# Cosformer attention and a low-rank mixer on one core: batch 1's loads without a gate, fewer zero matmuls at the start, one normalisation moved

## The chip, the cores and the metric

The kernel runs on one core of a Trainium2 chip. The metric is the device time of one execution in microseconds, as the median of several runs. The kernel before took 336.32 us as the median of 5 runs, which lay between 334.65 and 339.53 us.

## The reference

Two layers follow each other, for 8 batches of 576 positions. The first is a linear attention with 8 heads of 64 features, the second a token mixer of rank 32 with a channel network of 2048 hidden units.

```python
theta = np.pi / 2.0 * pos / S                       # S = 576
phi(x) = concat([relu(x) * cos(theta), relu(x) * sin(theta)])      # 64 -> 128 features
kv  = einsum('bhsf,bhsd->bhfd', phi(k), v);  z = sum(phi(k), axis=2)
x   = einsum('bhsf,bhfd->bhsd', phi(q), kv) / (einsum('bhsf,bhf->bhs', phi(q), z) + 1e-06)
u   = x + transpose(transpose(x) @ U @ V)           # mixes the 576 positions, rank 32
out = u + relu(u @ w_ch1) @ w_ch2                   # 512 -> 2048 -> 512
```

All inputs and the output are float32. The kernel computes in bfloat16 and accumulates in float32.

## The kernel before, in words

**Tiling.** A batch's 576 positions are four chunks of 128 (c = 0 to 3) and a tail of 64 (c = 4). The order ORD takes the tail first. Two consecutive batches form a pair, and their tails share one tile. The time goes to the channel network: `g1_main` is its first product (four matmuls of 512 columns for each of 16 blocks j of 128 hidden units), `g2_part` its second. For every batch but the first two, the attention is spread over slots between these products, by a plan written out as slot numbers.

**The order is written by hand.** Each engine works through its instructions in the order in which the program issues them, so a late operand holds all that is queued behind it on that engine. The loads of q, k and v are issued on the queue of SyncE (SP), one after the other. The weights w_ch1 (`w1_load`, four parts of 512 hidden units) and w_ch2 are loaded through the queue of GpSimd (POOL), which converts them to bfloat16 on the way.

**Batch 0** has nothing to hide behind. The stages are: zero matmuls on TensorE while the loads run (`keep_warm`, L669); `q_prep`, the scaled relu of q on VectorE (DVE) and ScalarE (ACT); five units of eight transposes each (`qtr_unit`, L673), each followed by one zero matmul and a copy out of PSUM; `k_prep`; thirteen zero matmuls (L677); then the chain. `chain_head` casts v, forms kv for heads 0 to 3, their denominators and reciprocals (`den_unit`, whose result is called rec), and normalises the five chunks for these heads (`xh_unit`: four small matmuls, then a multiplication on DVE). `chain_mid` does the same for heads 4 to 7, and puts between the second and the third of its five normalisations the opening of two products for the mixer (`uTd_open`, L646), the first half of the product with U (`A_unit`, L648) and its follow-up with V (`uTd_mm`, L650). `chain_end` does the second half of the product with U, which needs all five normalised chunks of heads 4 to 7.

**Batch 1** runs beside the sixteen blocks `g1_main(0, j)` of batch 0: after block j = 0 to 4 comes a `q_prep`, after j = 2 to 6 a `qtr_unit`, after j = 6 and 7 the `k_prep`, and after j = 7 the chain, in which `fill1` places the blocks j = 8 to 12.

**Gates.** Three small operations hold loads back. On POOL a copy of one element of k (L679 for batch 0, L715 for batch 1) stands ahead of the weight loads, so that these start only when k has landed. On SP a tiny transfer of one element of rec stands ahead of batch 1's nine loads (L685), and one of batch 1's rec ahead of batch 2's (L642, for b = 1). SP cannot issue what is behind such a transfer until rec exists. The buffers of q and v are single, so their next load also waits for the last reader; those of k are double.

Of the kernel before, what the change touches and what calls it, by code (L numbers as in the profile page):

```python
# [17 lines left out]
def kernel(  # L18
# [11 lines left out]
    nc = tc.nc  # L30
# [18 lines left out]
    def tail(b):  # L49
        lo = TS * (b % 2)  # L50
        return slice(lo, lo + TS)
# [37 lines left out]
    def w1_load(n):  # L89
        cs = slice(n * 512, n * 512 + 512)  # L90
        nc.gpsimd.dma_start(
            out=w1_bf[:, :, cs], in_=moe_w_ch1.rearrange("(d p) n -> p d n", p=P)[:, :, cs]
        )
# [7 lines left out]
    def cast(eng, o, i):  # L101
# [6 lines left out]
    V_, A_, G_ = nc.vector, nc.scalar, nc.gpsimd  # L108
# [9 lines left out]
        out=iota[:, 0:4], pattern=[[1, 4]], base=0, channel_multiplier=4,  # L118
        allow_small_or_imprecise_dtypes=True,
    )  # L120
    for lo in (0, TS):
        nc.gpsimd.iota(
            out=iota[lo : lo + TS, 4:5], pattern=[[1, 1]], base=512, channel_multiplier=1,
# [11 lines left out]
        out=stU[:, 0:4, :], in_=moe_U[0:512, :].rearrange("(p c) r -> p c r", c=4)  # L135
# [33 lines left out]
    def keep_warm(n, tag, bufs):  # L169
        w_ps = ps.tile([P, 512], FP32, tag=tag, bufs=bufs, name="w_ps")  # L170
        for _ in range(n):
            nc.tensor.matmul(out=w_ps, lhsT=zero[:, 0:P], rhs=zero, start=True, stop=True)  # L172
# [4 lines left out]
    mark2 = const.tile([1, 1], FP32)  # L177
# [13 lines left out]
    def v_prep(b, h0=0, h1=H, cs=range(5), engs=None):  # L191
        vx = v_ext[b % 2]
        for n, c in enumerate(cs):
            eng = engs[n] if engs else G_
            if eng is None:
                continue
            if c < 4:
                cast(eng, vx[:, c, h0:h1, 0:D], vst[b][:, h0:h1, c, :])
            else:
                cast(eng, vx[tail(b), 4, h0:h1, 0:D], vt[b][tail(b), h0:h1, :])  # L200

    def v_block(b, h0, h1, c0, c1, eng):
        cast(
            eng,
            v_ext[b % 2][:, c0:c1, h0:h1, 0:D].rearrange("p c h d -> p h c d"),
            vst[b][:, h0:h1, c0:c1, :],
        )
# [29 lines left out]
    def kv_unit(b, hg, tag, bufs, eng=None):  # L237
        if b not in kv_sb:
            kv_sb[b] = pool.tile([P, H, E], BF16, tag="kv", bufs=2, name="kv")
        acc = ps.tile([P, 4, E], FP32, tag=tag, bufs=bufs, name="kv_ps")  # L240
        vx = v_ext[b % 2]
        for i in range(4):
            h = hg * 4 + i
            for c in range(5):
                nc.tensor.matmul(  # L245
                    out=acc[:, i, :],
                    lhsT=k_p[b][:, c, h, :] if c < 4 else k_tl[:, h, :],
                    rhs=vx[:, c, h, :],
                    start=(c == 0),
                    stop=(c == 4),  # L250
                )
        cast(eng or V_, kv_sb[b][:, hg * 4 : hg * 4 + 4, :], acc)
# [32 lines left out]
    def qT_of(b, c, h):  # L285
        return q_pT[b][:, c, h, :] if c < 4 else q_tlT[:, h, :]

    def x_alloc(b):
        if b not in x_bf:
            x_bf[b] = pool.tile([P, 4, DM], BF16, tag="x_bf", bufs=2, name="x_bf")  # L290

    def x_of(b, c, rows=slice(0, P)):
        return x_bf[b][:, c, :] if c < 4 else x_tl[rows, :]

    def recip(rec, den):
        nc.vector.tensor_scalar(out=rec, in0=den, scalar1=1e-6, scalar2=None, op0=ALU.add)  # L296
        nc.vector.reciprocal(out=rec, in_=rec)  # L297

    def den_unit(b, h0, h1, tag, bufs):
        n = h1 - h0  # L300
        d_ps = ps.tile([P, 5, n], FP32, tag=tag, bufs=bufs, name="d_ps")
        for c in range(5):
            for h in range(h0, h1):
                nc.tensor.matmul(
                    out=d_ps[:, c, h - h0 : h - h0 + 1],
                    lhsT=qT_of(b, c, h),
                    rhs=kv_sb[b][:, h, D:E],
                    start=True,
                    stop=True,
                )  # L310
        rec = pool.tile([P, 5, n], FP32, tag="rec5", bufs=2, name="rec5")
        recip(rec, d_ps)
        return rec

    def xh_unit(b, c, h0, h1, rec, tag, bufs):
        x_alloc(b)
        n = h1 - h0
        rows = slice(0, P) if c < 4 else tail(b)
        acc = ps.tile([P, n, D], FP32, tag=tag, bufs=bufs, name="xh_ps")
        for h in range(h0, h1):  # L320
            nc.tensor.matmul(
                out=acc[:, h - h0, :], lhsT=qT_of(b, c, h), rhs=kv_sb[b][:, h, 0:D],
                start=True, stop=True,
            )
        nc.vector.tensor_tensor(
            out=x_of(b, c, rows)[:, h0 * D : h1 * D].rearrange("p (i d) -> p i d", d=D),
            in0=acc[rows],
            in1=rec[rows, c, :].unsqueeze(2).to_broadcast([P if c < 4 else TS, n, D]),
            op=ALU.mult,
        )  # L330
# [28 lines left out]
    def A_unit(b, tag, bufs, eng=None, n0=0, n1=DM, a_ps=None):  # L359
        if b not in A_sb:  # L360
            A_sb[b] = pool.tile([P, DM], BF16, tag="A_sb", bufs=2, name="A_sb")
        if a_ps is None:
            a_ps = ps.tile([P, DM], FP32, tag=tag, bufs=bufs, name="a_ps")
        for c in range(5):
            nc.tensor.matmul(  # L365
                out=a_ps[:, n0:n1],
                lhsT=U_of(b, c),
                rhs=x_of(b, c)[:, n0:n1],
                start=(c == 0),
                stop=(c == 4),  # L370
            )
        cast(eng or V_, A_sb[b][:, n0:n1], a_ps[:, n0:n1])
        return a_ps
# [37 lines left out]
    def uTd_open(b, d, tag, bufs, t=None):  # L411
        uT_alloc(b)
        if t is None:
            t = ps.tile([P, 4, P], FP32, tag=tag, bufs=bufs, name="uT_ps")
        uT_ps[b, d] = t
        for c in range(4):
            nc.tensor.matmul(
                out=t[:, c, :], lhsT=x_bf[b][:, c, d * P : d * P + P], rhs=ident,
                start=(c == 0), stop=False,
            )  # L420
# [5 lines left out]
    def uTd_evac(b, d, eng):  # L426
        cast(eng, uT[b][:, :, d, :], uT_ps[b, d])

    def uTd_mm(b, d):
        t = uT_ps[b, d]  # L430
        nc.tensor.matmul(
            out=t.rearrange("m c t -> m (c t)"), lhsT=A_sb[b][:, d * P : d * P + P],
            rhs=V_bf[:, 0:4, :].rearrange("r c t -> r (c t)"), start=False, stop=True,
        )
# [127 lines left out]
    ORD = (4, 0, 1, 2, 3)  # L562
# [54 lines left out]
    O2, G3 = ("o", 2), ("g", 3)  # L617

    def chain_head(b, fill, xt, engs):
        v_prep(b, 0, 4, (4,), (engs[0],))  # L620
        v_block(b, 0, 4, 0, 3, V_)
        v_block(b, 0, 4, 3, 4, engs[0])
        kv_unit(b, 0, "T", 1)
        fill(0)
        rec0 = den_unit(b, 0, 4, "X", 1)
        v_prep(b, 4, 8, (4,), (A_,))
        v_block(b, 4, 8, 0, 4, A_)
        fill(1)
        for n, c in enumerate(ORD):
            xh_unit(b, c, 0, 4, rec0, *xt[n])  # L630
            if n == 1:
                fill(2)
            if n == 3:
                kv_unit(b, 1, "T", 1, A_)
        return rec0

    def chain_mid(b, fill, xt, dt):
        fill(3)
        rec1 = den_unit(b, 4, 8, *dt)
        if b == 1:  # L640

            nc.sync.dma_start(out=mark2, in_=rec1[0:1, 0, 0:1])  # L642
        for n, c in enumerate(ORD[:2]):
            xh_unit(b, c, 4, 8, rec1, *xt[n])
        u01 = ps.tile([P, 2, 512], FP32, tag="X", bufs=1, name="u01")
        uTd_open(b, 0, None, None, u01[:, 0, :].rearrange("p (c t) -> p c t", c=4))  # L646
        uTd_open(b, 1, None, None, u01[:, 1, :].rearrange("p (c t) -> p c t", c=4))
        a0 = A_unit(b, "T", 1, A_, 0, 256)  # L648
        fill(4)
        uTd_mm(b, 0)  # L650
        uTd_mm(b, 1)
        uTd_evac(b, 0, A_)
        uTd_evac(b, 1, A_)
        for n, c in enumerate(ORD[2:]):
            xh_unit(b, c, 4, 8, rec1, *xt[2 + n])
        fill(5)
        return a0

# [7 lines left out]
        if m:  # L666
            keep_warm(m, *(O2 if n == 0 else G3))

    keep_warm(22, "X", 1)  # L669
    for c in TL:  # L670
        q_prep(0, c, (V_, V_ if c == 3 else A_))
    for n, c in enumerate(TL):
        qtr_unit(0, c, 0, H, (V_, A_, V_, A_, V_)[n], *(G3 if n < 3 else O2))  # L673
        keep_warm(1, "X", 1)
    for c in TL:
        k_prep(0, c, (V_, V_ if c == 3 else A_))
    keep_warm(13, "o", 2)  # L677
# [1 line left out]
    G_.tensor_copy(out=mark, in_=kt[0][0:TS, 0, 0:1])  # L679
    w1_load(0)  # L680
    cast_uv()
    rec0 = chain_head(0, warm0, (O2, O2, G3, G3, O2), (A_,))
    w1_load(1)

    nc.sync.dma_start(out=mark2, in_=rec0[0:1, 0, 0:1])  # L685
    alloc_q(1)
    load_main(qst[1], q, 1)
    load_tail(qt[1], q, 1)
# [100 lines left out]
```

## Time and profile before

| | |
|---|---|
| median of 5 runs | 336.32 us |
| the profiled execution's own time | 336.32 us |
| its span, first to last instruction | 334.6 us |
| TensorE matmul busy | 317.0 us (95%) |
| VectorE, ScalarE, GpSimd busy | 152.0, 163.8, 29.4 us |
| mean granted TensorE clock | 0.994 |
| HBM read and written | 36.86 and 9.44 MB |

The span is read from its own start. What lies around it, 1.7 us here, is part of the time but in no row. "PE" is TensorE's matmuls, "PEld" its weight loads, "SPq" the SP queue's issuing of transfers. The end of a matmul is modelled and overlaps the next, so the distance from one start to the next is a better measure of its cost than its own duration: a stream of matmuls of 512 columns advances by 0.216 us each at the full granted clock, though one is listed with 0.38 us. A few matmul records are missing from the trace.

### The profile page before, as it was taken

Reading aid. Unit: us, or ns where it says so; the run is one execution under the profiler, and the core shown is the slowest. Engines: PE = TensorE matmul, PEld = TensorE weight load, DVE = VectorE, ACT = ScalarE, POOL = GpSimd, SP = SyncE. Lnnn points to the kernel's source line nnn. Section 1 sums busy time; section 2 is a strip of 40 time slices with the busy share of each in tenths; the row PEclk is TensorE's granted clock in tenths of the full one; section 3 lists DMA queues with packets and bytes.
Section 4 is the critical chain, followed back from the end, with each engine's and each line's share of the span. In section 5 each row is a group of like instructions: output and inputs, shape, how many; then the busy total and the mean of one; then the engine's idle time right before and its main releaser. Section 6 shows DMA issues by size and latency. Waiting matters only on the chain.

```text
span 334.6 us, 5821 instructions
## 1 busy us (share of the span) xinstructions
PE 317.0 (95%) x2401; PEld 170.4 (51%) x2429; DVE 152.0 (45%) x334; ACT 163.8 (49%) x272; POOL 29.4 (9%) x60
## 2 busy tenths in 40 slices
PE   8998599999979989999999999999999999999995
PEld 3664365476545434556545444556455444464443
DVE  6766652682836863044725860255626520001211
ACT  4826745586936515655930476565900057660000
POOL 1312300200101010000011110000111100000000
PEclk9999989999999999999999999999999999999999
DMA  7979999929641414790389659901772230001131
GB/s 239 267 189 299 190 197 320 334 65 311 202 163 38 120 64 109 184 352 3 96 207 305 244 141 227 335 6 31 119 182 65 78 94 2 0 2 63 63 96 63
DMA packets 79054, 50.73 MB, mean 152 GB/s; under 512 B 47188, under 2 KB 76244, under 8 KB 79028
## 3 DMA queue, kind: packets, MB, share of 16 engines
q1 hardware_dynamic: 72596, 39.09, 41.5%
q0 software_dynamic: 6432, 11.27, 13.8%
q8 instruction: 19, 0.31, 0.4%
q14 instruction: 7, 0.06, 0.1%
HBM read 36.86 MB, written 9.44 MB: 138 GB/s over the span
## 4 chain that ended last, share of the span: by engine, by line
PE 65%; DVE 4%; issue 1%; ACT 1%; DVEq 0%
PE o_ps L518 29%; PE g_ps L466 25%; PE gt_ps L486 3%; PE va_ps L382 2%; PE kv_ps L245 2%; PE x_ps L339 2%; DVE k_p L213 2%; PE a_ps L365 2%; DVE o_sb L528 1%; PE t_ps L262 1%; DVE k_tl L213 1%; DVE rec L297 0%; ACT k_p L211 0%; DVE x_bf L349 0%; DVE rec L296 0%
## 5 line engine op out<-in xcount | busy, mean ns | idle before, releaser
L466 PE MATMUL g_ps<-uT,w_bf 128*128 128x512 bf16 x512 | 120.3, 382 | 0.1
L475 ACT ACTIVATE hid<-g_ps 128x512 bf16<-128x512 f32 x128 | 76.2, 596 | 85.7 <-PE g_ps L466 85.6
L518 PE MATMUL o_ps<-w_bf,hid 128*128 128x512 bf16 (+1 forms) x510 | 116.2, 372 | 1.4 <-DVE o_sb L528 0.5
L518 PEld LDWEIGHTS <-hid 128*128 128x128 bf16 x528 | 49.9, 98 | 53.6 <-issue 1.6
L466 PEld LDWEIGHTS <-w_bf 128*128 128x128 bf16 x512 | 48.7, 98 | 54.5 <-issue 0.8
L528 DVE TENSOR_TENSOR o_sb<-u_bf,o_ps 128x512 f32<-128x512 bf16 (+1 forms) x33 | 22.0, 668 | 67.9 <-PE o_ps L518 67.8
L538 POOL DMA_DIRECT2D out_dram<-o_sb x24 | 13.4, 557 | 177.7 <-DVE o_sb L528 160.6
L383 DVE TENSOR_TENSOR u_bf<-x_bf,va_ps 128x512 bf16<-128x512 bf16 x32 | 21.9, 686 | 10.2 <-PE va_ps L382 9.8
L105 DVE CAST kv<-kv_ps 128x260 bf16<-128x260 f32 x14 | 6.0, 428 | 37.4 <-PE kv_ps L245 37.4
L211 ACT ACTIVATE q_p<-qst,sinw 128x512 bf16<-128x512 f32 x29 | 20.4, 710 | 4.3 <-DMA qst<-in_q_dram 4.2
L349 DVE TENSOR_TENSOR x_bf<-x_ps,rec 128x512 bf16<-128x512 f32 x24 | 16.6, 691 | 0.8
L103 ACT ACTIVATE v_ext<-vst 128x512 bf16<-128x512 f32 (+2 forms) x23 | 14.8, 653 | 2.8 <-DMA vst<-in_v_dram 2.7
L486 PE MATMUL gt_ps<-uT_tl,w_bf 128*128 128x128 bf16 x256 | 16.1, 219 | 0.0
L486 PEld LDWEIGHTS <-w_bf 128*128 128x128 bf16 x256 | 15.1, 98 | 1.4
L172 PE MATMUL w_ps<-zero 128*128 128x512 bf16 x44 | 13.7, 445 | 1.5 <-DVE halfpi L142 1.2
L518 PE MATMUL o_ps<-w_bf,hid_tl 128*128 128x512 bf16 x62 | 15.0, 379 | 0.1
L382 PE MATMUL va_ps<-A_sb,V_bf 128*128 128x512 bf16 x38 | 14.4, 379 | 0.6 <-DVE A_sb L105 0.5
L245 PE MATMUL kv_ps<-v_ext,k_p 128*128 128x65 bf16 x256 | 12.0, 193 | 3.0 <-DVE v_ext L105 2.7
L245 PEld LDWEIGHTS <-k_p 128*128 128x128 bf16 x256 | 11.2, 97 | 6.8 <-ACT k_p L211 3.5
L213 DVE TENSOR_SCALAR k_p<-kst,cosw 128x512 bf16<-128x512 f32 x28 | 13.4, 492 | 0.1
L339 PEld LDWEIGHTS <-q_pT 128*128 128x128 bf16 x192 | 9.1, 98 | 8.2 <-DVE x_bf L349 1.6
L296 DVE TENSOR_SCALAR rec<-x_ps 128x8 f32<-128x8 f32 (+1 forms) x30 | 4.9, 164 | 17.0 <-PE x_ps L339 16.9
(99 smaller groups left out, 262.0 us busy)
## 6 DMA issues: line engine op xcount, KB each, us to landing
qst<-in_q_dram SPq DMA_DIRECT2D x8, 1024.0 KB, 7.6
kst<-in_k_dram SPq DMA_DIRECT2D x8, 1024.0 KB, 7.7
vst<-in_v_dram SPq DMA_DIRECT2D x6, 1024.0 KB, 9.3
out_dram<-o_sb POOLq DMA_DIRECT2D x24, 256.0 KB, 2.7
w_bf<-in_moe_w_ch_dram POOLq DMA_DIRECT2D x8, 512.0 KB, 9.8
vst<-in_v_dram SPq DMA_DIRECT2D x4, 512.0 KB, 7.1
out_dram<-o_sb SPq DMA_DIRECT2D x7, 256.0 KB, 2.3
qt<-in_q_dram SPq DMA_DIRECT2D x8, 128.0 KB, 8.1
```

The costliest lines, as they stand in the source:

```text
L211: nc.scalar.activation(out=o, in_=i, func=AF.Relu, bias=0.0, scale=w)
L213: eng.tensor_scalar(out=o, in0=i, scalar1=0.0, scalar2=w, op0=ALU.max, op1=ALU.mult)
L245: nc.tensor.matmul(out=acc[:, i, :], lhsT=k_p[b][:, c, h, :] if c < 4 else k_tl[:, h, :], rhs=vx[:, c, h, :], start=(c == 0), stop=(c == 4),)
L339: nc.tensor.matmul(out=acc[:, g, i * E : i * E + E], lhsT=qT_of(b, c, h), rhs=kv_sb[b][:, h, :], start=True, stop=True,)
L349: nc.vector.tensor_tensor(out=x_of(b, c, rows).rearrange("p (g i d) -> p g i d", g=2, d=D), in0=view[:, :, :, 0:D], in1=rec[rows].unsqueez ...
L382: nc.tensor.matmul(out=va, lhsT=V_bf[:, c, :], rhs=A_sb[b], start=True, stop=True)
L383: nc.vector.tensor_tensor(out=u_bf[b][:, c, :] if c < 4 else u_tl[b // 2][rows, :], in0=x_of(b, c, rows), in1=va[rows, :], op=ALU.add,)
L466: nc.tensor.matmul(out=g_ps.rearrange("p (c t) -> p c t", c=4), lhsT=w1_bf[:, d, j * P : j * P + P], rhs=uT[b][:, :, d, :], start=(d == 0) ...
L475: nc.scalar.activation(out=hid[b][:, j, :], in_=g_ps, func=AF.Relu, bias=0.0, scale=1.0)
L486: nc.tensor.matmul(out=g_ps[:, jj, :], lhsT=w1_bf[:, d, j * P : j * P + P], rhs=uT_tl[pr][:, d, :], start=(d == 0), stop=(d == 3),)
L518: nc.tensor.matmul(out=o[:, cols], lhsT=lhs[:, j, c * P : c * P + P], rhs=w2_bf[:, j, cols], start=(j == 0), stop=(j == NJ - 1),)
L528: nc.vector.tensor_tensor(out=o_sb[:, cols], in0=u[:, cols], in1=o[:, cols], op=ALU.add)
```

## The change

It has three parts. First, the gate on SP ahead of batch 1's loads (L685) is removed, so these follow batch 0's loads and those of U and V directly. Second, the zero matmuls at the start are 18 instead of 22, and those between the transposes follow only the second and the fourth unit instead of all five. Third, in `chain_mid` of batch 0 three normalisations instead of two stand ahead of the mixer's products, and two instead of three behind them; batch 1 keeps two and three. The gate ahead of batch 2's loads stays.

```diff
     def chain_mid(b, fill, xt, dt):
         fill(3)
+        m = 3 if b == 0 else 2
         rec1 = den_unit(b, 4, 8, *dt)
...
-        for n, c in enumerate(ORD[:2]):
+        for n, c in enumerate(ORD[:m]):
             xh_unit(b, c, 4, 8, rec1, *xt[n])
...
-        for n, c in enumerate(ORD[2:]):
-            xh_unit(b, c, 4, 8, rec1, *xt[2 + n])
+        for n, c in enumerate(ORD[m:]):
+            xh_unit(b, c, 4, 8, rec1, *xt[m + n])
...
-    keep_warm(22, "X", 1)
+    keep_warm(18, "X", 1)
...
         qtr_unit(0, c, 0, H, (V_, A_, V_, A_, V_)[n], *(G3 if n < 3 else O2))
-        keep_warm(1, "X", 1)
+        if n in (1, 3):
+            keep_warm(1, "X", 1)
...
-    rec0 = chain_head(0, warm0, (O2, O2, G3, G3, O2), (A_,))
+    chain_head(0, warm0, (O2, O2, G3, G3, O2), (A_,))
     w1_load(1)
-
-    nc.sync.dma_start(out=mark2, in_=rec0[0:1, 0, 0:1])
     alloc_q(1)
     load_main(qst[1], q, 1)
     load_tail(qt[1], q, 1)
```

More of the change, by code (lines that the diff above doesn't have):

```diff
@@ L634, in chain_head @@
                 kv_unit(b, 1, "T", 1, A_)
-        return rec0
     def chain_mid(b, fill, xt, dt):
         fill(3)
+        m = 3 if b == 0 else 2
         rec1 = den_unit(b, 4, 8, *dt)
```

## The prediction

> **What bounds the kernel now.** The page comes first: TensorE is busy for 95% of the span, and the slices show where it is not.
>
> ```profile
> span 334.6 us, 5821 instructions
> PE 317.0 (95%) x2401; PEld 170.4 (51%) x2429; DVE 152.0 (45%) x334; ACT 163.8 (49%) x272; POOL 29.4 (9%) x60
> PE   8998599999979989999999999999999999999995
> PEclk9999989999999999999999999999999999999999
> DMA  7979999929641414790389659901772230001131
> ```
>
> A slice is 8.4 us. The first five slices are not full, and the granted clock dips in the sixth. The change touches just these slices, and from some 53 us on TensorE is full but for waits of some 5 us around 90 to 120 us, which hang on ACT and DVE and on nothing changed. So what the start gains, the end should gain. The list of waits names the causes:
>
> ```profile
> DVE q_tl L213 <- DMA qt<-in_q_dram: 2.3, 1, 2.3
> PEld L262 <- ACT q_tl L211: 1.9, 1, 1.9
> PE kv_ps L245 <- DVE v_ext L105: 2.7, 1, 2.7
> SPq L685 <- DVE x_tl L325: 6.0, 1, 6.0
> ```
>
> Read from below: SP stood 6.0 us in the gate, the tail of batch 1's q came late to DVE, and batch 1's first transposes came late to TensorE. TensorE's timeline places that, and the last number of a line is its idle time:
>
> ```profile
> 1.19 7.36 PE L172 MATMUL w_ps<-zero 128*128 128x512 bf16 x22 [1.19 <-DVE halfpi L142]
> 8.39 0.61 PE L262 MATMUL t_ps<-ident,q_p 128*128 128x128 bf16 x8
> 12.10 2.97 PE L172 MATMUL w_ps<-zero 128*128 128x512 bf16 x12 [0.23 <-ACT q_pT L103]
> 15.14 0.28 PE L245 MATMUL kv_ps<-v_ext,k_p 128*128 128x65 bf16 x4
> ...
> 24.69 2.32 PE L466 MATMUL g_ps<-uT,w_bf 128*128 128x512 bf16 x10
> 28.40 0.62 PE L262 MATMUL t_ps<-ident,q_tl 128*128 128x128 bf16 x8 [1.39 <-ACT q_tl L211]
> ...
> 37.84 0.25 PE L245 MATMUL kv_ps<-v_ext,k_p 128*128 128x65 bf16 x3 [2.72 <-DVE v_ext L105]
> ```
>
> And the stages, with the granted clock and the DMA share at the end of each line:
>
> ```profile
> 16.50:19.50 3.00, 2.79 (x85) 2.48 (x86) 2.20 (x7) 0.39 (x1) 1.43 (x4) 1.00 0.14 13
> 27.01:28.40 1.39, 0.00 (x1) 0.01 (x1) 0.74 (x2) 0.75 (x2) 0.00 (x0) 1.00 1.10 371
> 40.00:44.00 4.00, 4.00 (x34) 1.96 (x32) 1.36 (x5) 0.80 (x2) 0.00 (x0) 0.57 1.19 190
> ```
>
> The gate leaves the DMA engines empty for 2.6 us (3.00 x 0.86). The third line is a clock loss after the idle stretch at 35 to 38 us.
>
> **Zero matmuls.** Before the change the first transposes start at 8.39, though ACT ended the first sine part of q at 7.36 (6.65 + 0.71): the zero matmuls are in the way. Late in their run they advance by 0.216 each, so four fewer free TensorE 0.86 earlier, at 7.53. The units then take 0.44 each and are held by the preps: ACT ends its parts at 7.36, 7.98, 8.60 and 9.22, DVE its at 9.13. I get unit starts at 7.53, 8.03, 8.69, 9.13 and 9.79 instead of 8.39, 9.05, 9.71, 10.38 and 11.04, the end near 10.4. DVE then copies the last unit at 10.42 instead of 11.69 and could start k at 10.84 instead of 12.03. Main k is there (issued 2.07, landed 8.6 later, 10.67), the tail before 11.38, when POOL's gate on it opened. ACT is the tighter one: it cannot copy unit 1 before its q work ends at 9.22, two copies of 1.02 end at 11.1, and its k work starts then instead of at 11.95, 0.9 earlier. The thirteen zero matmuls wait for the same copy, so they go from 12.10 to 11.2 too. Before, they, ACT's cast of v (14.70 + 0.41) and DVE's (14.54 + 0.55) all end within 0.1 us of the first kv matmul at 15.14; all now come 0.9 to 1.2 earlier. Main v of heads 0 to 3 lands at 12.94 (6.04 + 6.9), that of heads 4 to 7 at 14.32 (7.02 + 7.3), needed at 14.4. **-0.9 us.** The bounds are -1.2 (DVE's lead) and +1.7, worked out under the rivals, if the clock is lost. The row that opposes a loss is the idle 1.39 at 27.01, after which the clock stayed 1.00; the new hole, 10.4 to 11.2, is shorter. I take -0.9.
>
> **Third normalisation ahead.** Its four matmuls take 0.13 (0.53 for twelve, less overlap) and now precede the mixer's product, whose follow-up at 21.25 waits for ACT's cast: 0.13 late there, 0.13 back in the later group. In return DVE, idle 1.13 before 22.02, does one multiplication (0.35 from start to start) in that idle time. Two are left instead of three, and DVE ends them at 22.8 instead of 23.11. The second product with U, at 22.51, stretched to 0.92 instead of 0.60 because it waits for these. **-0.27 us**, between +0.13 (DVE not the last) and -0.35. The PSUM buffers are taken in the same order as before.
>
> **No gate: when the loads land.** The listing of transfers gives the time from issue to landing as its last number; here q's tail of batch 1 and the two weight parts of w1, the first with batch 0's v, the second in the hole:
>
> ```profile
> qt<-in_q_dram SPq DMA_DIRECT2D x1, 128.0 KB, 8.7
> w_bf<-in_moe_w_ch_dram POOLq DMA_DIRECT2D x1, 512.0 KB, 5.7
> w_bf<-in_moe_w_ch_dram POOLq DMA_DIRECT2D x1, 512.0 KB, 5.6
> ```
>
> SP ends issuing U at 12.06, so q of batch 1 goes at about 12.1 instead of 18.46; its buffer's last reader ended at 9.22, and v's readers (16.38 before) are through when SP gets there. POOL's queue is not moved, but the transfers share the DMA engines: in 10 to 16.5 us these are full, so 6.4 us of earlier issue is not 6.4 us of earlier landing. Bound from below: the first q load, on empty engines, took 5.8 us, so 17.9. From above: all that landed before q's tail at 27.65 (18.95 + 8.7) still lands, less the 2.6 us hole, so 25.05. I plan with the upper end. In the same way k comes by 29.3, v by 32.0 (27.72 + 6.9 - 2.6). The needs: in before's own time, ACT turns to q's tail after its first hidden block at 26.78, which the two steps above make 25.6; k is needed near 31.5 and v near 34.5. All land in time.
>
> **What that is worth.** Not 1.39 + 2.72. Below are before's times, with the shift of 1.17 left out. ACT's sine part of the tail runs 26.7 to 27.4 behind the first hidden block, so the transposes start at 27.45 instead of 28.40: 0.95 won, 0.45 stays as a wait, for ACT's order now and not for the load. From there TensorE alternates transposes and blocks by 1.31 each. ACT's last block before k waited 0.71 for TensorE (33.85), so ACT's k work, which runs without a hole from there to 38.25, moves by the same 0.95. DVE, by its durations, ends the casts of v at 36.5 instead of 37.70: 1.2. The kv matmuls of chunk 3 waited for ACT's k until 38.31, so **-0.95 us** counts. The 2.7 us wait is mostly work of DVE and ACT after the last transposes and stays at about 2.5. Bounds: 0 (loads no earlier) and -1.55, if ACT's order costs nothing.
>
> **The sum.** 0.9 + 0.27 + 0.95 = 2.1 us. The profiled run took 336.3, the median too, so I forecast **334.2 us**, with the clock loss at 40 us kept. That loss is the large unknown: eight blocks' matmuls advanced by 0.43 instead of 0.216 there, 1.6 to 1.7 us. The stretch without 512-column matmuls before it is 5.06 us long (34.95 to 40.01) and about 5.0 in my schedule.
>
> The Trainium skill, page "TensorE: Matmul & The Clock Gate", section "HAM oscillation — how this bites in real kernels", wants no idle gap on TensorE above about 3.4 us. The trace loses its clock after 2.9 us idle and some sparse matmuls, so the measurement is the stricter one. By the page the 0.8 us hole costs nothing and the loss at 40 us would be gone, for 332.6; by the row it stays, for 334.2.
>
> **Rivals.**
>
> *The clock loss at 40 us goes* because the windows in which the clock is set fall otherwise: 334.2 - 1.6 = 332.6. The lowest of the five runs, 334.65, is 1.7 below the median, so it may come and go. Against it: the sparse stretch is as long as before. Chance 0.17.
>
> *The loads take the engines from the weights*, slower. Place: block j = 4 of batch 0 needs the second w1 part, at 30.16 before and 28.05 in my schedule. It is issued at 17.15 and took 5.6 us in the hole that the gate made; now all of q, k and v is queued ahead in time. If SP's queue had the engines first, w1 would land with the last of v, at 32.0, a stall of 3.95 and a total of +1.85: 338.1. It decides from a landing at 30.2. For it: w2's loads took up to 16.9 us in company. Against: the first w1 part shared its time with v of batch 0 and took 5.7. Chance 0.1. The page "DMA: Bandwidth & Descriptors", section "Queues, rings and completion order", says an engine takes turns between queues, which would give some 24.5 and no stall; no row here tells turns from precedence.
>
> *The zero matmuls were needed.* If the clock halves at 11 us, the thirteen take 5.6 instead of 2.8 and end at 16.8 instead of 14.0, 1.7 after 15.14: 336.3 + 1.7 - 0.27 - 0.95 = 336.8. Chance 0.1.
>
> *The start gains nothing more*, because v or k is later when q of batch 1 is near: -1.2 is left, 335.1. Chance 0.13. *The gate wasn't what held the loads* (full queues do): q lands as before, -1.17 alone, also 335.1; in it the 27.63 would stand. Chance 0.05.
>
> **How the numbers follow.** Forecast 0.45 at 334.2, by the bounds 333.0 to 335.3. A measurement of this kernel tells about 1% (3.4 us) from no change, so 332.95 and 339.7 are the limits. Faster: the first rival and a little of the forecast, 0.22. Slower by that much needs two of the bad cases together: 0.08. The rest, 0.70. The range leaves out less than 0.2: 331.8 to 338.0.
>
> **What would show it.** Right: first kv matmul near 14.2, q's first issue near 12.1 and DMA share full through 16.5 to 19.5, transposes of batch 1 near 26.3 with a wait under 0.5, kv of batch 1 near 35.5 to 36.2, everything after 2.1 earlier. Wrong: a clock below 1.00 before 20 us, a wait of the blocks for w1, or q's tail after 25.6.

## The result, and the profile after

The changed kernel takes 335.45 us (median of 51 runs, 334.18 to 337.07) against 337.25 us for the kernel before (median of 93 runs, 334.65 to 340.37). The ratio is 0.9947, with a 95% interval of 0.9935 to 0.9959: 1.8 us less. The forecast was 2.1 us less and a time of 334.2; the kernel before itself was 0.9 us slower in the longer series than in the five runs it was made from. Executions that were disturbed or took over 1.5% more than the fastest of their kernel are left out of all ratios and of the groups below (of before, 340.13 and 479.92 us).

The two profiled executions do not show this gain. That of the changed kernel took 336.53 us, among the slowest of its runs, and that of before 336.32, among the fastest. Its page:

```profile
span 334.8 us, 5804 instructions
PE 316.6 (95%) x2394; PEld 170.6 (51%) x2422; DVE 152.2 (45%) x334; ACT 163.9 (49%) x272; POOL 29.5 (9%) x60
PE   8889599999979989999999999999999999999995
PEclk9999789999999999999999999999999999999999
DMA  7999999919541414990389759901462230001131
```

The dip of the granted clock (PEclk) begins a slice earlier than before and is deeper. TensorE's timeline shows where the lead is won and where it is lost:

```profile
1.19 6.66 PE L172 MATMUL w_ps<-zero 128*128 128x512 bf16 x18 [1.19 <-DVE halfpi L142]
7.68 1.06 PE L262 MATMUL t_ps<-ident,q_p 128*128 128x128 bf16 x16
14.43 0.29 PE L245 MATMUL kv_ps<-v_ext,k_p 128*128 128x65 bf16 x4 [0.36 <-DVE v_ext L105]
...
22.47 0.61 PE L417 MATMUL uT_ps<-ident,x_bf 128*128 128x128 bf16 x8
23.90 0.60 PE L466 MATMUL g_ps<-uT,w_bf 128*128 128x512 bf16 x2 [0.83 <-DMA w_bf<-in_moe_w_ch_dram]
...
27.67 0.62 PE L262 MATMUL t_ps<-ident,q_tl 128*128 128x128 bf16 x8 [0.57 <-ACT q_tl L211]
...
37.29 0.53 PE L245 MATMUL kv_ps<-v_ext,k_p 128*128 128x65 bf16 x4 [2.90 <-DVE v_ext L105]
```

The first kv matmul starts at 14.43 instead of 15.14, 0.71 earlier. The opening of the mixer's last two products starts at 22.47 instead of 23.38, 0.91 earlier. Then there is a wait that the kernel before did not have: the first hidden block stands still for the first part of w1, and starts at 23.90 instead of 23.82. The whole lead is gone. From there the early q wins 0.73 at the transposes (27.67 instead of 28.40) and 0.55 at batch 1's kv. The stages, with the granted clock and the DMA share near the end of each line, show what becomes of that:

```profile
16.50:19.50 3.00, 2.86 (x82) 2.60 (x82) 2.61 (x10) 0.39 (x1) 1.88 (x4) 1.00 1.14 245
37.00:44.00 7.00, 6.19 (x65) 3.78 (x66) 2.09 (x8) 2.83 (x5) 0.00 (x0) 0.52 1.21 194
```

The DMA engines are busy through 16.5 to 19.5 us (1.14, where it was 0.14). A mean clock of 0.52 over 7.00 us is 6.7 us at half speed (0.48 x 7.00 / 0.5). In the profile of before it is 0.57 over the 4.00 us from 40 to 44, so 3.4 us. I call 3.4 us at half a window: before has one here, the changed kernel two. At 56.62 the next blocks are 0.12 us behind those of before (56.50).

The mean granted clock of an execution tells how many such windows it had, since 3.4 us at half take 0.005 off the mean over some 335 us: 0.993 to 0.995 is one, 0.988 to 0.990 two, 0.983 to 0.984 three. Runs in each group, with their mean time in us:

| kernel | no window | one | two | three |
|---|---|---|---|---|
| before, in the runs made beside the experiments | 0 | 26: 336.19 | 41: 337.38 | 18: 339.50 |
| changed | 0 | 23: 335.14 | 41: 335.89 | 0 |

At an equal number of windows the changed kernel is 1.0 to 1.5 us faster, and it has no run with three. Most of these runs were not made side by side; in the series in which both kernels ran beside each other ("beside the next three" below) it is 1.0 us with one window and 1.7 with two. The experiments were made to tell which part of the change does that.

### The profile page after: what moved, and what is told of

It is laid out like the page before. It is cut to its first block, busy times and chain, and to the rows that moved or that the text cites. A ratio compares the mean times of both kernels' runs of the same rounds, so it can differ in the third digit from the quotient of the medians.

```text
span 334.8 us, 5804 instructions
## 1 busy us (share of the span) xinstructions
PE 316.6 (95%) x2394; PEld 170.6 (51%) x2422; DVE 152.2 (45%) x334; ACT 163.9 (49%) x272; POOL 29.5 (9%) x60
## 3 DMA queue, kind: packets, MB, share of 16 engines
q1 hardware_dynamic: 72594, 39.09, 41.3%
## 4 chain that ended last, share of the span: by engine, by line
PE 65%; DVE 4%; issue 1%; ACT 1%; DVEq 0%
PE o_ps L518 29%; PE g_ps L466 25%; PE gt_ps L486 3%; PE va_ps L382 2%; PE kv_ps L245 2%; PE x_ps L339 2%; DVE k_p L213 2%; PE a_ps L365 2%; DVE o_sb L528 1%; PE t_ps L262 1%; DVE k_tl L213 1%; DVE rec L297 0%; ACT k_p L211 0%; DVE x_bf L349 0%; DVE rec L296 0%
## 5 line engine op out<-in xcount | busy, mean ns | idle before, releaser
L172 PE MATMUL w_ps<-zero 128*128 128x512 bf16 x37 | 11.9, 464 | 1.8 <-DVE halfpi L142 1.2
L213 DVE TENSOR_SCALAR k_p<-kst,cosw 128x512 bf16<-128x512 f32 x28 | 13.3, 491 | 0.4 <-DMA kst<-in_k_dram 0.3
## 6 DMA issues: line engine op xcount, KB each, us to landing
w_bf<-in_moe_w_ch_dram POOLq DMA_DIRECT2D x8, 512.0 KB, 11.4
```

Source lines behind the costliest of these rows:

```text
L213: eng.tensor_scalar(out=o, in0=i, scalar1=0.0, scalar2=w, op0=ALU.max, op1=ALU.mult)
```

## The experiments

**The gate alone removed** (zero matmuls and normalisations as before):

```diff
     rec0 = chain_head(0, warm0, (O2, O2, G3, G3, O2), (A_,))
     w1_load(1)
-    nc.sync.dma_start(out=mark2, in_=rec0[0:1, 0, 0:1])
```

> The gate ahead of batch 1's loads is removed, the zero matmuls and the order of the normalisations stay as before. Theory (each part is worth what was forecast, and they collide at w1's first part): without the gate w1's first part lands near 23.6 us instead of 17.2, which just meets the first hidden block at 23.8, so no wait for it or one under 0.3 us; q's tail lands near 25 us, the first transposes of batch 1 start near 27.5 instead of 28.4, and the time falls by 0.7 to 0.95 us (ratio 0.997 to 0.998). Rival A (the gate's removal is worth nothing, all of the gain is in the zero matmuls): ratio 1.000. Rival B (the half-clock windows decide): the time goes with the mean granted clock of the runs, whatever the kernel.

Measured: 335.44 us against 336.50, ratio 0.9968 (0.9946 to 0.9990). Six runs have one window (mean 334.73; before, beside it, 336.02), five two (336.12; 336.77), none three. This part alone gives 1.1 us by the ratio, 0.3 to 1.8 by the interval, and the rival that it is worth nothing falls. So does the rival that the number of windows decides alone: the kernel is faster at an equal number. No line of its profile is used, since in that execution the zero matmuls advanced by 0.83 us each instead of 0.216.

**The zero matmuls alone** (18 and two, the gate kept):

```diff
-    keep_warm(22, "X", 1)
+    keep_warm(18, "X", 1)
...
-        keep_warm(1, "X", 1)
+        if n in (1, 3):
+            keep_warm(1, "X", 1)
```

> Only the zero matmuls are fewer (18 instead of 22, two instead of five between the transposes). Theory: the first kv matmul of batch 0 at 14.2 to 14.4 instead of 15.1, and 0.7 to 0.9 us less at the end (ratio 0.997 to 0.998), no clock below 1.00 before 30 us. Rival A: all of the measured gain is here, 1.8 us (ratio 0.9947). Rival C (the zero matmuls hold the clock): a clock under 1.00 in the first 20 us and a ratio of 1.000 or more.

Measured: 337.01 us against 336.50, ratio 1.0009 (0.9979 to 1.0038). Nothing arrives at the end, at equal numbers of windows either (one: 336.11 against 336.02 of before; two: 336.78 against 336.77). TensorE's timeline tells why:

```profile
23.03 0.59 PE L466 MATMUL g_ps<-uT,w_bf 128*128 128x512 bf16 x2
23.46 0.59 PE L431 MATMUL uT_ps<-V_bf,A_sb 128*128 128x512 bf16 x2
23.89 2.32 PE L466 MATMUL g_ps<-uT,w_bf 128*128 128x512 bf16 x10
28.48 0.62 PE L262 MATMUL t_ps<-ident,q_tl 128*128 128x128 bf16 x8 [2.27 <-ACT q_tl L211]
```

The first kv matmul is at 14.34 and the first hidden block at 23.03, 0.8 earlier than before, as expected. But q's tail still lands at 27.65 (issued 18.15, 9.5 later), where it landed before, although it was issued 0.8 earlier. The wait for it grows from 1.39 to 2.27 us, and the transposes start at 28.48 against 28.40. The lead is swallowed whole. That wait, longer than any other here before these transposes, was followed by no loss of clock. The clock stays 1.00 up to 36 us, so the zero matmuls taken out were not holding it.

**The normalisation alone.**

```diff
+        m = 3 if b == 0 else 2
...
-        for n, c in enumerate(ORD[:2]):
+        for n, c in enumerate(ORD[:m]):
```

> Only the third normalisation of batch 0's heads 4 to 7 stands ahead of the mixer's products. Theory: the second product with U is shorter by 0.2, the first hidden block starts 0.27 us earlier, ratio 0.999, which five rounds can hardly tell from 1. Rival: the later follow-up with V takes it back, ratio 1.000.

Measured: 336.43 us, ratio 1.0001 (0.9969 to 1.0033); the expected 0.27 us lies inside that interval, so its worth at the end is not shown. Its profiled execution, at 338.96 us, was one with three windows, and shows where the third one lies:

```profile
26.40:28.40 2.00, 0.05 (x1) 0.00 (x0) 0.57 (x2) 0.60 (x1) 0.00 (x0) 1.00 1.10 348
28.40:32.30 3.90, 3.73 (x23) 2.27 (x24) 2.40 (x6) 2.52 (x5) 1.28 (x3) 0.62 1.16 283
...
40.00:46.00 6.00, 5.33 (x53) 3.13 (x54) 1.74 (x5) 2.19 (x4) 0.00 (x0) 0.50 1.22 196
```

TensorE stood for 2.1 us before the transposes (first line), and the clock that follows is 0.62 over the next 3.9 us. So the wait for q, which the gate lengthens, is at times followed by a half-clock window (here after 2.12 us; not after the 2.27 us of the run before this one).

**Zero matmuls and normalisation changed, the gate kept.** The edit is the two diffs above.

> Zero matmuls and normalisation as in the changed kernel, the gate kept. Theory: w1's first part lands by 18 and is not waited for, so the lead at the first hidden block is the full 0.9 to 1.2 us; it reaches the end but for what q's late tail takes (the gate itself moves with rec, 0.7 earlier), 0.7 to 1.2 us less (ratio 0.9965 to 0.998), and the changed kernel is faster than this one by about 0.7 us. Rival A: same as the changed kernel, ratio 0.995. Rival D (the gate's removal costs, since w1 waits): this one is faster than the changed kernel, ratio under 0.994.

Measured: 336.95 us, ratio 1.0009 (0.9983 to 1.0035). The theory, that the lead of some 1.1 us reaches the end, fails, and with it the rival that removing the gate costs time. In the mean of the runs with two windows it is at 336.94, before at 336.77. The one profiled execution did reach the transposes at 27.30 and ended 1.1 us before that of before, with one window (here q's tail, issued 1.2 us earlier, did land 1.2 us earlier, at 26.5), but only one run in eleven was like it: eight had two windows and two had three. The three kernels that keep the gate have 9 runs of 35 with three windows; the changed kernel and the one without the gate have none in 75.

**The changed kernel beside the next three.** No edit.

> The changed kernel again, on the chip of the next three. Ratio to before 0.9935 to 0.9965, no run with a mean granted clock of 0.984 (three half-clock windows), which the kernels with the gate showed in 13 of 69 runs and those without it in none of 63. If the gate's absence is not what removes them, some appear here.

Measured: 335.72 us against 338.28, ratio 0.9925 (0.9897 to 0.9952); six runs with one window, six with two, none with three. In this profile the first part of w1 is in time, since it lands 9.9 us after its issue, and the second is not:

```profile
14.56 0.29 PE L245 MATMUL kv_ps<-v_ext,k_p 128*128 128x65 bf16 x4 [0.88 <-DVE v_ext L105]
...
23.04 0.59 PE L466 MATMUL g_ps<-uT,w_bf 128*128 128x512 bf16 x2
...
26.80 0.62 PE L262 MATMUL t_ps<-ident,q_tl 128*128 128x128 bf16 x8 [0.57 <-ACT q_tl L211]
29.23 1.04 PE L466 MATMUL g_ps<-uT,w_bf 128*128 128x512 bf16 x4 [0.50 <-DMA w_bf<-in_moe_w_ch_dram]
```

The first line shows a second leak in the lead: TensorE was ready 0.88 us before DVE had cast v, because DVE had stood 0.90 us for k. Batch 0's k was there only at 11.3 to 11.8 in six of the twelve later profiles, not at 10.67.

**A gate that opens earlier**, at the first kv instead of rec:

```diff
     mark2 = const.tile([1, 1], FP32)
+    mark3 = const.tile([1, 1], BF16)
...
     w1_load(1)
+    nc.sync.dma_start(out=mark3, in_=kv_sb[0][0:1, 0, 0:1])
     alloc_q(1)
```

> The changed kernel with a gate again, but one that opens 2 us earlier than before's: it waits for the first kv (cast by DVE near 15.7) instead of rec. Theory (without a gate w1's first part takes the place of q as the load that is late, so the earlier transposes are lost in the wait for w1): w1's first part lands by 20 and the 0.8 us wait of the first hidden block is gone; q's tail lands at 25.5 to 26.5, so batch 1's first transposes start near 26.6 instead of 27.7 and the time is 0.5 to 1 us below the changed kernel's. Rival (the loads as a whole set the pace, whichever comes first): what w1 gains q loses, the same time as the changed kernel within 0.3 us or more, and half-clock windows as in before.

Measured: 339.89 us over all twelve runs and 338.64 over the eight that enter the ratio, 1.0013 to before (0.9969 to 1.0057): some 2.9 us above the changed kernel. A part of it is the slower rival of the prediction, at the place named there:

```profile
27.15 0.62 PE L263 MATMUL t_ps<-ident,q_tl 128*128 128x128 bf16 x8 [0.69 <-ACT q_tl L212]
27.61 1.03 PE L467 MATMUL g_ps<-uT,w_bf 128*128 128x512 bf16 x4
28.47 0.61 PE L263 MATMUL t_ps<-ident,q_p 128*128 128x128 bf16 x8
30.76 1.04 PE L467 MATMUL g_ps<-uT,w_bf 128*128 128x512 bf16 x4 [1.67 <-DMA w_bf<-in_moe_w_ch_dram]
```

(Lines are one further down in this kernel.) The first part of w1 lands in 6.3 us, as the theory has it, but the second takes 12.0 and lands at 30.7, batch 1's q having gone into the queues 1.8 us before it. The expectation counted the first part only.

But this kernel is slower elsewhere too, far from its gate. At 50 us its profile is 2.4 us behind that of the changed kernel beside it, and another 2.4 us are lost in one place at 200 us, where TensorE waits for ACT, and ACT had stood for a later batch's v (issue to landing 13.3 us, against 9.0 to 11.2 in the kernels without mark3). The profile page's line of these products ends in their idle time and what ended most of it; the changed kernel comes first, then this one:

```profile
L466 PE MATMUL g_ps<-uT,w_bf 128*128 128x512 bf16 x512 | 120.2, 382 | 0.5 <-DMA w_bf<-in_moe_w_ch_dram 0.5
L467 PE MATMUL g_ps<-uT,w_bf 128*128 128x512 bf16 x512 | 120.7, 383 | 3.9 <-ACT hid L476 2.3
```

The transfers of SP's queue (q1) hold the DMA engines longer throughout, for the same 39.09 MB. In the same order:

```profile
q1 hardware_dynamic: 72594, 39.09, 42.1%
q1 hardware_dynamic: 72596, 39.09, 47.5%
```

In the other undisturbed profiles that share is 41.0 to 44.0%, and in the one other kernel with mark3 (both edits, below) 48.8%. The gate acts once, at 16 us, and so hardly explains this. The edit also adds a tile of one bfloat16 element (mark3), which may shift the buffers allocated after it; whether that slows the transfers was not tested. So this run doesn't show what an earlier gate by itself would do.

**Twelve zero matmuls in TensorE's hole** before batch 1's kv, in the changed kernel:

```diff
+        if b == 1:
+            keep_warm(12, "X", 1)
         kv_unit(b, 0, "T", 1)
```

> The changed kernel with 12 more zero matmuls (2.6 us) in TensorE's hole before batch 1's first kv. Theory (the half-clock windows at 37 to 44 us come of the hole and cost 0.8 to 1.7 us each): most runs have a mean clock above 0.995 and the time is 1.0 to 2.5 us below the changed kernel's. Rival (the sparse small matmuls after the hole are enough to lose the clock): one window less at most, 0 to 0.8 us less. If the zero matmuls last longer than the hole, up to 0.5 us more.

Measured: 333.82 us (333.30 to 334.31), ratio to before 0.9869 (0.9825 to 0.9913), a mean clock of 0.999 to 1.000 in all six runs. It is 1.9 us below the changed kernel beside it and faster than both kernels of this study. The stages:

```profile
34.00:37.00 3.00, 2.88 (x14) 1.08 (x12) 2.94 (x8) 2.98 (x6) 0.69 (x1) 1.00 1.24 204
37.00:46.00 9.00, 8.25 (x139) 5.95 (x140) 4.33 (x13) 4.65 (x9) 0.00 (x0) 1.00 1.20 191
```

The hole is filled and the clock does not fall. So the hole is the cause of the late windows: the sparse matmuls behind it, which are still there, are not enough. The windows cost 1.9 us between them in the mix of one and two that the changed kernel has; against its runs with one window beside it (335.41) it is 1.6, against those with two (336.17) 2.3.

**Both edits together.**

> Both of the edits above. If they are independent, the gains of the two add up: 1.5 to 3.5 us below the changed kernel. If the earlier gate gives nothing, the same as with the zero matmuls alone.

Measured: 338.37 us, ratio 1.0009 (0.9972 to 1.0045); five runs without a window, six with one and one with two. What the zero matmuls win is gone, but the wait for w1 (0.48 us in this profile, 0.20 with the zero matmuls alone) is the smaller part of that. At full clock this profile ends 4.3 us behind, of which 0.5 are lost by 48 us and 2.7 in the wait for ACT at 201 us. Like the kernel with the earlier gate alone, it has mark3 and its longer transfers, so it tells nothing sure of the gate either.

**The gate alone removed, with the twelve zero matmuls**, which takes the late windows out of the comparison.

> The gate removed alone (zero matmuls at the start and normalisations as before), with the 12 zero matmuls in the hole that steady the clock. Against the changed kernel with the same 12, which gave 333.8: if the fewer zero matmuls and the moved normalisation are taken back by the wait for w1 (theory), the same within 0.3 us; if they are worth the 1.2 us of the forecast, 1.0 to 1.2 us slower than that, 335.

**The kernel before, with the twelve zero matmuls.**

> The kernel before with the 12 zero matmuls in the hole, the gate kept. Theory (the gate costs twice: the wait for q of 1.4 to 2.3 us, and now and then a half-clock window after it): the windows at 37 to 46 us go, the one after the wait for q at 28 to 32 us can stay (mean clock 0.995 in some runs, 1.000 in others); 1 to 2 us below the kernel before, and 1 to 2 us above the same edit without the gate. If the gate costs nothing but those late windows, the same as without the gate.

These two ran beside each other. Without the gate: 334.30 us, ratio to before 0.9905 (0.9873 to 0.9938), the clock at 1.000 in all six runs. With the gate: 335.94 us, 0.9948 (0.9917 to 0.9978). The gate's removal is worth 1.6 us by the medians. The two intervals overlap a little, but five of the six runs without the gate are faster than each of the twelve with it. The runs with the gate fall into two halves: six at a clock of 0.998 to 1.000 with a mean of 334.97 us, and six at 0.995 with 337.25. The profiled one is of the latter kind. First its transposes of batch 1, then those of the kernel without the gate, then its stages:

```profile
28.69 0.65 PE L262 MATMUL t_ps<-ident,q_tl 128*128 128x128 bf16 x8 [1.94 <-ACT q_tl L211]
```

```profile
27.51 0.62 PE L262 MATMUL t_ps<-ident,q_tl 128*128 128x128 bf16 x8 [0.57 <-ACT q_tl L211]
```

```profile
26.40:28.40 2.00, 0.35 (x2) 0.00 (x0) 0.48 (x1) 0.60 (x2) 0.00 (x0) 1.00 1.09 376
28.00:33.00 5.00, 4.31 (x25) 2.40 (x26) 3.17 (x7) 3.04 (x5) 0.95 (x3) 0.66 1.14 304
37.00:46.00 9.00, 8.08 (x112) 4.86 (x112) 5.81 (x16) 6.27 (x11) 0.00 (x0) 1.00 1.23 201
```

A wait of 1.94 us before the transposes, then the clock at 0.66, and later 1.00. This separates the two prices of the gate: 0.5 us in the runs without a window (334.97 against a mean of 334.50 without the gate), and 2.3 us more in those with one. By an estimate, some 1.7 of the 2.3 are the window itself (3.4 us at half the clock); the rest may be a longer wait (1.94 us here, 1.39 in the profile of before), which the other runs, having no profile, don't show. As for the other two parts, the changed kernel with the same twelve matmuls is at 333.82 in the run beside other kernels, its interval (0.9825 to 0.9913) overlaps this one's (0.9873 to 0.9938), and so 0 to 1.2 us for them stays open. In the two profiles only 0.2 us of them is left (batch 1's last mixer products open at 48.40 against 48.57, the spans are 332.2 and 332.4 us): TensorE waits 0.20 us for w1 in the changed kernel and not at all in the other.

**The gate between the loads of q and of k**: q goes at once, k and v wait for rec, in the changed kernel.

```diff
     load_tail(qt[1], q, 1)
+    nc.sync.dma_start(out=mark2, in_=rec0[0:1, 0, 0:1])
     alloc_k(1)
```

> The changed kernel with the gate on rec put back between the loads of q and of k: q goes at once, k and v of batch 1 at 17.5. Theory (k and v in the queue are what holds w1's second part, q's 1.2 MB what holds its first): w1's first part lands at 20 to 22 and the second 5.5 to 8 us after its issue, at 23 to 26, so no wait for w1; q's tail stays near 23; k lands near 29 to 31, needed at 32. 0.3 to 0.8 us below the changed kernel. Rival (the engines are full either way): k or v is late instead and batch 1's first kv comes 1 us or more later, slower than the changed kernel.

**The same with the twelve zero matmuls.**

> The same with the 12 zero matmuls in the hole. If the two edits are independent, 0.3 to 0.8 us below the changed kernel with zero matmuls, near 333.2, with a mean clock of 0.999 or 1.000.

Measured: 335.89 us, 0.9949 (0.9928 to 0.9971), and, in four runs, 333.81 us, 0.9880 (0.9841 to 0.9918): neither is told from the same kernel without this gate. The theory fails on w1's second part, which still took 11.9 and 11.4 us and was waited for (0.92 and 0.45 us). In this kernel k is issued only 0.1 us behind that part of w1, where before it was 2.5 us behind, so k is not excluded as a cause; but taking k and v out from in front of w1 did not help, and q's load, issued 4.8 us ahead, is the likelier one. No run separates the two further.

## Why the prediction was right, and where it was not

The sign and the size were right, 1.8 us measured against 2.1, and the range held. That the sum came out is in good part luck: the two terms of 0.9 and 0.27 us hardly reach the end, and the gate's term is larger than forecast by a loss of clock that the prediction had left out. One of its own signs of being wrong did come, a wait of the blocks for w1 (0.83 us), and batch 1's kv came at 37.29 where 35.5 to 36.2 was named.

*Zero matmuls, -0.9.* The steps up to the transposes hold: the first starts at 7.68 (forecast 7.53), the thirteen zero matmuls at 11.11 (11.2), and no clock is lost. What failed is "Main k is there": its landing of 10.67 came from one execution, and where k lands at 11.3 or later DVE waits for it (0.33 to 1.36 us in five of the nine profiles with fewer zero matmuls). The first kv starts at 13.86 to 14.96 in those nine, median 14.58, and at 14.79 to 15.14 in the four with all zero matmuls, median 14.97: some 0.4 us are won there, not 0.9. And what is won does not reach the end. With the gate, q's tail did not land earlier for being issued earlier in the profile of the zero matmuls alone, and the wait for it took the lead; in time nothing is left (ratio 1.0009 alone, and 1.0009 with the normalisation). Without the gate the wait for w1 takes some of it: 0.20 to 0.92 us in five profiles with the lead, none in the one without it. The prediction worked out -0.9 and -0.95 as if they added; it said itself that the engines are full up to 16.5 us, but took that into account only for batch 1's loads.

*Third normalisation, -0.27.* The second product with U takes 0.72 instead of 0.92, so 0.2 us of it is seen in the trace. At the end it is too small to be resolved (ratio 1.0001).

*No gate: when the loads land.* Right: q's tail lands at 25.25 (13.35 + 11.9) against the 25.05 planned, SP issues q at 12.74 against 12.1, the hole in the DMA is gone. k lands at 30.7 and not by 29.3, still in time.

*What that is worth, -0.95.* The order of ACT does what was said: 0.57 us of wait are left at the transposes where 0.45 was forecast, in all six profiles in which q's load has no gate. In time the gate's removal gave 1.1 us alone, from which 0.95 can't be told, and 1.6 with the late windows steadied. The missing part is the half-clock window after the wait for q. The prediction put "the clock stayed 1.00" after the idle 1.39 as a row against clock losses; in two other executions with the gate (normalisation alone, and before with twelve zero matmuls) the same wait lasted 2.12 and 1.94 us and a window did follow. That is the term left out. In the pair with steadied late windows it is the larger part of the gain: the runs with a window, half of them, are 2.3 us slower, against 0.5 us in all.

*The late clock loss.* Forecast "kept", and it was kept; one window was assumed, and 41 of 64 runs have two. The price of one, 1.6 to 1.7 us worked out from the matmuls, agrees with the 1.6 between the changed kernel's runs with one window and the same kernel with the hole filled; a second window costs it less, 0.75 between its groups of one and two.

*The rival "the loads take the engines from the weights"* had 0.1. Its wait is there in four of the six profiles in which q's load has no gate, on the second part at block j = 4 (0.50, 0.20, 0.92, 0.45 us), and, not forecast, on the first part in the profiled execution (0.83). What it got wrong is the size: w1's second part lands at 28.4 to 30.0, not at 32.0, and so it takes a part of the gain and not more. The Trainium skill, page "DMA: Bandwidth & Descriptors", section "Queues, rings and completion order", has an engine take turns between queues. The prediction's estimate by that page was a landing near 24.5; the measured 28.4 to 30.0 lie between this and the 32.0 of full precedence of SP's queue.

## What to carry to other kernels

Ask of each load on the start path not only when it is issued, but what it displaces: where the DMA engines are full, an earlier issue of one load is a later landing of another (w1's first part took 11.7 us in the changed kernel instead of 5.7), and a lead won ahead of the slowest load ends in the wait for it. Where TensorE waits for 2 us or more, count the clock that it may lose afterwards as well as the wait; a dozen zero matmuls in a hole that cannot be closed were worth about as much here (1.9 us in the changed kernel, 1.7 in the kernel before) as the three edits together (1.8). One profiled execution gives one landing time per load: batch 0's k landed between 10.1 and 11.8 us, so take a slack of 1 us as uncertain. An edit that adds a buffer can change more than the order of things: compare the share of the DMA queues before believing it. And compare kernels by groups of runs with the same granted clock.

## What was not expected of the hardware

How long w1's second part takes goes with whether it or batch 1's q reached the queues first. From the listings of transfers, one execution each, issue times in us, w1 through POOL's queue, q through SP's:

| kernel | lead of w1 over q at issue | w1's second part, issue to landing |
|---|---|---|
| before | 1.31 (17.15, 18.46) | 5.6 |
| zero matmuls and normalisation, gate kept | 0.88 | 5.3 |
| normalisation alone | 0.65 | 6.9 |
| zero matmuls alone | 0.54 | 7.3 |
| before with twelve zero matmuls | 0.02 | 9.5 |
| gate at the first kv, alone and with zero matmuls (transfers longer throughout) | -1.81, -1.79 | 12.0, 10.7 |
| gate alone removed, with twelve zero matmuls | -4.79 | 10.8 |
| changed, with twelve zero matmuls | -4.83 | 11.0 |
| gate between q and k, alone and with zero matmuls | -4.82, -4.84 | 11.9, 11.4 |
| changed (profiled, and beside the others) | -4.86, -4.99 | 11.1, 11.3 |

A lead of about 1 us goes with half of the time to landing that a lag of nearly 5 us does. Except with the gate between q and k, batch 1's k follows q by 1.2 to 1.3 us, so the table doesn't tell q's share from that of k. The gate of the kernel before, as it happened, gave w1 this lead; without the gate, w1 takes twice as long and just misses or just meets its use.

The clock fell after waits of 1.94 and 2.12 us, and did not after 2.27 us in a third profile; in the kernel before with zero matmuls in the late hole, six of twelve runs have the clock of one window and six none. Where it fell, it was to half (0.50 in the slices inside), for 3.4 us or twice that: 0.66 over 5.00 us is 3.4, 0.52 over 7.00 us is 6.7. The Trainium skill, page "TensorE: Matmul & The Clock Gate", section "HAM oscillation — how this bites in real kernels", asks for no idle gap above about 3.4 us; the runs here show that on this kernel 2 us can be too long.
